# Five loads moved to the front of the load queue of an attention and MLP kernel

## The chip, the cores and the metric

The kernel runs on one core of a Trainium2 chip. The metric is device time in microseconds (us) of one execution: the median of three runs is 648.29 us (647.89 to 649.43). A further execution, the one that was profiled, took 646.66 us; durations in the text come from it.

## The reference

Attention with a soft cap over 4 batches, 12 heads, 448 positions and 64 numbers per head, then a two-layer MLP with a squared ReLU over the 1792 resulting rows (768 wide, 2048 in the middle):

```python
scores = scale * np.matmul(q, k.transpose(0, 1, 3, 2))
scores = cap * np.tanh(scores / cap)
scores = scores - np.max(scores, axis=-1, keepdims=True)
attn = np.exp(scores)
attn = attn / (np.sum(attn, axis=-1, keepdims=True) + 1e-09)
x = np.matmul(attn, v)              # then heads side by side: (1792, 768)
h = x @ w_in
r = np.maximum(h, 0.0)
out = (moe_s * (r * r) + moe_b) @ w_out
```

Everything is float32, `cap` is a scalar that comes from memory, and the result is (1792, 768) in float32.

## The kernel before

Two heads make a pair, and a batch has six pairs. For a pair the kernel loads k and q (128 x 448 float32, 224 KB each) and v (256 KB). TensorE computes scores in pieces of 128 keys for both heads (L514, four or eight matmuls into a `ps_s` buffer, of which there are two). ScalarE takes a piece through tanh (L518) and then exp (L522). The tanh needs the scale `tsc`, which VectorE computes from `cap` (L1163, L1164, the function `setup`). TensorE then multiplies the exponentials with v (L573) and with ones for the sums (L581), and ScalarE copies the result out of PSUM (L611).

The MLP weights are prepared in the same time. `w_in` is read in 24 chunks of 128 x 1024 32-bit words (512 KB, the halves of float64 numbers): the function `piece` joins the two words of each number into a float32. One of its steps goes either to ScalarE (one instruction at L687) or to VectorE (L681 and L682); the others, L675 and L678, are on VectorE. Sums of squares follow (L723 to L725) and, after all three chunks of a column group, small matmuls (L735), a VectorE step (L743 to L745) and a matmul that spreads its result over the lanes (L479). Later the weights are split into two float16 halves and multiplied with the attention output; that fills most of the run, but lies behind the part that this change touches.

The order of work is set by the class `Plan`. All operations are recorded with a duration and a rank; `emit` simulates the engines, picks at each step the operation that can start first, and writes the chosen indices to the list `out`. At the end it calls the operations in the order of `out`, so each engine's instructions stand in a fixed order and are run in it. All loads are issued by SyncE (SP) on one queue. Eight completion semaphores serve these transfers in turn, so that in the stretch treated here SP issues a load only after the eighth load before it has landed. The 16 DMA engines work through the queue in the order of issue, apart from small differences between them.

On TensorE six matmuls on a zeroed tile (L1191) come first, to give the engine work at the start; the scores of the first pair follow.

Of the kernel before, what the change touches and what calls it, by code (L numbers as in the profile page):

```python
# [23 lines left out]
class Plan:  # L24
# [55 lines left out]
    def emit(self):  # L80
# [40 lines left out]
        ran = [None] * n  # L121
# [45 lines left out]
        out = []  # L167
        todo = n
        while todo:
# [25 lines left out]
            t, i, e = best  # L195
# [41 lines left out]
                            free[q][x] = max(free[q][x], last[k] + 0.15)  # L237
            out.append(i)
            todo -= 1
        for i in out:  # L240
            self.ops[i][0][ran[i]][1]()


def arrange(units, at):

    key = {}
    for name, pre, _ in units:
# [4 lines left out]
CHOICE = {  # L252
    'bias': 3.969,
    'shy': {'DVE': 0.3, 'POOL': 0.5},
# [42 lines left out]
    'ahead': 0.3,  # L297
    'tail': 0.9,
    'expo': ('ACT', 'DVE'),
    'evac': ('ACT',),  # L300
    'sq': ('ACT', 'DVE', 'POOL'),
    'whi': ('ACT', 'DVE'),
# [990 lines left out]
```

## Time and profile before

| what | value |
|---|---|
| median of 3 runs | 648.29 us |
| the profiled execution | 646.66 us |
| its span, first to last instruction | 644.8 us |
| TensorE busy | 621.4 us, 96% |
| VectorE / ScalarE / GpSimd busy | 441.9 / 341.6 / 201.3 us |
| mean granted TensorE clock | 0.995 |

Some 1.9 us of the profiled execution lie outside its span. Times in the views count from the first instruction of the span. Busy shares are means over the whole run; this change concerns the first 30 us alone, where ScalarE and VectorE are nearly always busy and the DMA engines are too.

### The profile page before, as it was taken

Reading aid. Unit: us, or ns where it says so; the run is one execution under the profiler, and the core shown is the slowest. Engines: PE = TensorE matmul, PEld = TensorE weight load, DVE = VectorE, ACT = ScalarE, POOL = GpSimd, SP = SyncE. Lnnn points to the kernel's source line nnn. Section 1 sums busy time; section 2 is a strip of 40 time slices with the busy share of each in tenths; the row PEclk is TensorE's granted clock in tenths of the full one; section 3 lists DMA queues with packets and bytes.
Section 4 is the critical chain, followed back from the end, with each engine's and each line's share of the span. In section 5 each row is a group of like instructions: output and inputs, shape, how many; then the busy total and the mean of one; then the engine's idle time right before and its main releaser. Section 6 shows DMA issues by size and latency. Waiting matters only on the chain.

```text
span 644.8 us, 11247 instructions
## 1 busy us (share of the span) xinstructions
PE 621.4 (96%) x4308; PEld 327.6 (51%) x4308; DVE 441.9 (69%) x891; ACT 341.6 (53%) x459; POOL 201.3 (31%) x176
## 2 busy tenths in 40 slices
PE   4999999999999899989999999999999999999997
PEld 1333334344444333333444445555557996555997
DVE  4998888996887799798978691446667221666322
ACT  3999988966675478476668460314334001433100
POOL 2031434282571477566524320016014000010000
PEclk9999999999999999989999999999999999999999
DMA  8855644631614664764483424366012874100772
GB/s 294 314 145 190 232 121 152 215 124 60 214 28 134 218 202 137 243 190 139 146 307 132 160 103 156 127 228 222 3 32 76 263 257 146 49 1 1 225 239 80
DMA packets 54774, 101.67 MB, mean 158 GB/s; under 512 B 16192, under 2 KB 34752, under 8 KB 54720
## 3 DMA queue, kind: packets, MB, share of 16 engines
q1 hardware_dynamic: 54720, 100.95, 47.0%
q8 instruction: 34, 0.56, 0.3%
q14 instruction: 20, 0.16, 0.1%
HBM read 82.58 MB, written 18.17 MB: 156 GB/s over the span
## 4 chain that ended last, share of the span: by engine, by line
PE 76%; DMA 10%; DVE 7%; SPq 2%; POOL 2%; issue 2%; ACT 1%; POOLq 0%; ACTq 0%; DVEq 0%
PE ps_m L1031 9%; PE ps_v L573 7%; PE ps_s L514 7%; PE ps_s L1031 6%; PE ps_s L871 6%; PE ps_s L873 6%; PE ps_s L872 6%; PE ps_m L871 5%; PE ps_m L872 5%; PE ps_m L873 5%; PE ps_m L1122 4%; PE ps_m L1123 4%; PE ps_m L1124 4%; PE ps_v L581 3%; DMA w<-in_w_out 3%; DMA bed<-in_qT 2%
## 5 line engine op out<-in xcount | busy, mean ns | idle before, releaser
L1031 PEld LDWEIGHTS <-w 128*128 128x128 f16 x1008 | 96.6, 98 | 1.1
L518 ACT ACTIVATE bed<-ps_s,arena 128x896 f32<-128x896 f32 x84 | 81.2, 1004 | 21.7 <-PE ps_s L514 17.5
L514 PE MATMUL ps_s<-bed 64*128 64x448 f32 (+1 forms) x384 | 82.4, 592 | 9.8 <-DMA bed<-in_qT 6.8
L522 ACT ACTIVATE bed<-bed,par 128x896 f32<-128x896 f32 x84 | 85.6, 1042 | 0.4
L573 PE MATMUL ps_v<-bed 128*32 128x448 f32 x768 | 82.6, 552 | 0.8 <-ACT pw L611 0.7
L1123 PE MATMUL ps_m<-gt,w 128*128 128x448 f16 x192 | 67.7, 352 | 0.7 <-POOL gt L446 0.7
L871 PE MATMUL ps_m<-x,w 128*128 128x448 f16 x192 | 67.8, 353 | 0.2 <-DVE arena L640 0.2
L1122 PE MATMUL ps_m<-gt,w 128*128 128x448 f16 x192 | 67.8, 353 | 0.0
L871 PE MATMUL ps_s<-x,w 128*128 128x448 f16 x192 | 67.7, 352 | 0.0
L872 PE MATMUL ps_s<-x,w 128*128 128x448 f16 x192 | 67.7, 352 | 0.0
L1124 PE MATMUL ps_m<-gt,w 128*128 128x448 f16 x192 | 67.7, 352 | 0.0
L873 PE MATMUL ps_s<-x,w 128*128 128x448 f16 x192 | 67.7, 352 | 0.0
L872 PE MATMUL ps_m<-x,w 128*128 128x448 f16 x192 | 67.7, 352 | 0.0
L873 PE MATMUL ps_m<-x,w 128*128 128x448 f16 x192 | 67.7, 352 | 0.0
L966 ACT ACTIVATE pw<-ps_s,arena 128x448 f32<-128x448 f32 x32 | 20.2, 633 | 88.6 <-PE ps_s L873 88.3
L871 PEld LDWEIGHTS <-w 128*128 128x128 f16 x384 | 37.5, 98 | 40.4 <-issue 6.3
L514 PEld LDWEIGHTS ps_s<-bed 64*128 64x128 f32 (+1 forms) x384 | 27.9, 180 | 54.9 <-issue 25.9
L873 PEld LDWEIGHTS <-w 128*128 128x128 f16 x384 | 37.6, 98 | 35.1
L872 PEld LDWEIGHTS <-w 128*128 128x128 f16 x384 | 37.6, 98 | 33.5 <-issue 0.2
L446 POOL TENSOR_TENSOR bed<-bed 128x896 f32<-128x896 f32 (+2 forms) x25 | 45.5, 1821 | 6.2 <-PE ps_v L573 4.6
L573 PEld LDWEIGHTS ps_v<-bed 128*32 128x32 f32 x768 | 21.0, 110 | 49.7 <-issue 32.5
L445 DVE TENSOR_TENSOR pw<-pw 128x224 f32<-128x224 f32 x53 | 25.1, 494 | 27.5 <-ACT pw L970 24.9
(142 smaller groups left out, 1022.8 us busy)
## 6 DMA issues: line engine op xcount, KB each, us to landing
w<-w SPq DMA_DIRECT2D x48, 512.0 KB, 4.4
w<-in_w_out SPq DMA_DIRECT2D x24, 512.0 KB, 5.8
w<-ws SPq DMA_DIRECT2D x24, 512.0 KB, 4.7
w<-in_w_in SPq DMA_DIRECT2D x18, 512.0 KB, 5.6
bed<-in_v SPq DMA_DIRECT2D x24, 256.0 KB, 3.8
ws<-w SPq DMA_DIRECT2D x12, 512.0 KB, 3.3
bed<-in_kT SPq DMA_DIRECT2D x24, 224.0 KB, 3.7
bed<-in_qT SPq DMA_DIRECT2D x24, 224.0 KB, 3.9
```

The costliest lines, as they stand in the source:

```text
L446: "POOL": (0.1 + n * 0.00225, lambda: nc.gpsimd.tensor_tensor(dst(), a(), c(), op)),
L514: nc.tensor.matmul(P[kp][o, h, 0:S], keys, P[q][rows], start=True, stop=True)
L518: 1.01, rank, lambda: nc.scalar.activation(P[kh], P[kp][:, :, 0:S], AF.Tanh, scale=tsc[:, 0:1]),
L522: 1.04, rank, lambda: nc.scalar.activation(P[kh], P[kh], AF.Exp, scale=par[:, 0:1]), r=["par"], w=[kh],
L573: nc.tensor.matmul(P[kp][o, 0, 0:S], P[kv][:, c, o], prob(c, h), start=(c == 0), stop=(c == NC))
L871: nc.tensor.matmul(ps[:, 0:S], wh, x[:, 0], start=(c == 0), stop=False)
L872: nc.tensor.matmul(ps[:, 0:S], wh, x[:, 1], start=False, stop=False)
L873: nc.tensor.matmul(ps[:, 0:S], wl, x[:, 0], start=False, stop=(c == NP - 1))
L1031: nc.tensor.matmul(at(), w(g, zw), b(g, zb), start=g == 0 and x == 0, stop=g == n - 1 and x == 2,)
L1122: nc.tensor.matmul(ps[:, 0:S], wh, ghi[:, f], start=(f == 0), stop=False)
L1123: nc.tensor.matmul(ps[:, 0:S], wh, glo[:, f], start=False, stop=False)
L1124: nc.tensor.matmul(ps[:, 0:S], wl, ghi[:, f], start=False, stop=(f == NF - 1))
```

## The change

After the simulation, the loads of `cap` and of k and q of the first two pairs are called first, in that order, and then everything else in the order it had. The simulated schedule is not made again.

```diff
-        for i in out:
+        lead = [i for k in CHOICE["lead"] for i in out if k in self.ops[i][3] and ran[i] == "SP"]
+        for i in lead + [i for i in out if i not in lead]:
             self.ops[i][0][ran[i]][1]()
...
     'expo': ('ACT', 'DVE'),
+    'lead': (('par', 0), ('k', 0, 0), ('q', 0, 0), ('k', 0, 1), ('q', 0, 1)),
     'evac': ('ACT',),
```

The start of SP's queue before (`gt` holds the first chunks of w_in, `bed` k, q and v, `par` the three scalars):

```order
L667 DMA gt<-in_w_in 128x1024 x2
L496 DMA bed<-in_v 128x512 x2
L1168 DMA par<-in_cap 128x1
L490 DMA bed<-in_kT 128x448 x2
L492 DMA bed<-in_qT 128x448
L667 DMA gt<-in_w_in 128x1024
L492 DMA bed<-in_qT 128x448
L667 DMA gt<-in_w_in 128x1024
L1168 DMA par<-in_s 128x1
L1168 DMA par<-in_b 128x1
L667 DMA w<-in_w_in 128x1024 x3
```

And now (lines count two more here):

```order
L1170 DMA par<-in_cap 128x1
L492 DMA bed<-in_kT 128x448
L494 DMA bed<-in_qT 128x448
L492 DMA bed<-in_kT 128x448
L494 DMA bed<-in_qT 128x448
L669 DMA gt<-in_w_in 128x1024 x2
L498 DMA bed<-in_v 128x512 x2
L669 DMA gt<-in_w_in 128x1024 x2
L1170 DMA par<-in_s 128x1
L1170 DMA par<-in_b 128x1
L669 DMA w<-in_w_in 128x1024 x3
```

Five loads moved ahead of two w_in chunks and two v loads, and q of the second pair also ahead of the third w_in chunk. From the fourth w_in chunk on, the same loads stand in front of each load.

VectorE's queue before, at its start (`gt` w_in chunks, `arena` small values such as tsc):

```order
L681 TENSOR_SCALAR gt<-gt 128x512
L682 SCALAR_TENSOR_TENSOR gt<-gt 128x512
L675 TENSOR_SCALAR gt<-gt 128x512 x2
L678 SCALAR_TENSOR_TENSOR gt<-gt 128x512 x2
L1163 RECIPROCAL arena<-par 128x1
L1164 TENSOR_SCALAR arena<-arena 128x1
```

And now:

```order
L683 TENSOR_SCALAR gt<-gt 128x512
L684 SCALAR_TENSOR_TENSOR gt<-gt 128x512
L677 TENSOR_SCALAR gt<-gt 128x512 x2
L680 SCALAR_TENSOR_TENSOR gt<-gt 128x512 x2
L1165 RECIPROCAL arena<-par 128x1
L1166 TENSOR_SCALAR arena<-arena 128x1
```

Nothing moved: the two instructions that make tsc stand behind the work on the first two w_in chunks, as they did. The same holds for ScalarE, TensorE and GpSimd, whose queues are word for word those of before apart from line numbers; ScalarE's begins with this (`ps_s` scores):

```order
L689 ACTIVATE gt<-gt 128x512
L1183 ACTIVATE arena<-par 128x1
L520 ACTIVATE bed<-ps_s,arena 128x896
L689 ACTIVATE gt<-gt 128x512
L524 ACTIVATE bed<-bed,par 128x896
L520 ACTIVATE bed<-ps_s,arena 128x896 x2
```

The first tanh (L520 here, L518 before) has a step of the second w_in chunk ahead of it, and the first exp has a step of the fourth.

## Rows read from the trace of the kernel before

**Rows 1.** The chain that ended last, in time order, 0 to 100 us: start, us, what.

```profile
5.59 7.52 DMA bed<-in_qT
...
13.12 7.17 DMA gt<-in_w_in
...
27.94 0.16 PE ps_m L479
28.11 1.65 PE ps_v L573 x16
...
71.08 1.73 PE ps_s L514 x8
```

**Rows 2.** Timeline, cap's issue and ScalarE: start, us, engine, line, operation [idle before <-releaser].

```profile
2.59 0.43 SPq L1168 DMA_DIRECT2D par<-in_cap  x1
...
5.59 0.71 ACT L687 ACTIVATE gt<-gt 128x512 f32<-128x512 f32 x1 [3.58 <-DMA gt<-in_w_in]
...
9.46 0.20 ACT L1181 ACTIVATE arena<-par 128x1 f32<-128x1 f32 x1 [3.16 <-DMA par<-in_cap]
...
13.25 1.01 ACT L518 ACTIVATE bed<-ps_s,arena 128x896 f32<-128x896 f32 x1 [3.59 <-PE ps_s L514]
14.47 0.69 ACT L687 ACTIVATE gt<-gt 128x512 f32<-128x512 f32 x1 [0.21 <-DMA gt<-in_w_in]
15.06 1.02 ACT L522 ACTIVATE bed<-bed,par 128x896 f32<-128x896 f32 x1
16.00 1.87 ACT L518 ACTIVATE bed<-ps_s,arena 128x896 f32<-128x896 f32 x2
```

**Rows 3.** Timeline of VectorE, 0 to 21 us.

```profile
5.94 1.28 DVE L678 SCALAR_TENSOR_TENSOR gt<-gt 128x512 int32<-128x512 int32 x2
...
9.66 0.15 DVE L1164 TENSOR_SCALAR arena<-arena 128x1 f32<-128x1 f32 x1
...
12.53 0.43 DVE L681 TENSOR_SCALAR gt<-gt 128x512 f32<-128x512 f32 x1 [2.65 <-DMA gt<-in_w_in]
...
20.32 0.43 DVE L681 TENSOR_SCALAR gt<-gt 128x512 f32<-128x512 f32 x1 [0.37 <-DMA gt<-in_w_in]
```

**Rows 4.** Stretches of 1 us: window, PE, PEld, DVE, ACT, POOL busy, PEclk, DMA share, GB/s.

```profile
6.00:7.00 1.00, 0.00 (x0) 0.00 (x0) 1.00 (x3) 0.30 (x1) 0.30 (x1) 1.00 0.55 197
7.00:8.00 1.00, 0.00 (x0) 0.00 (x0) 0.23 (x1) 0.00 (x0) 1.00 (x1) 1.00 0.22 68
8.00:9.00 1.00, 0.00 (x0) 0.00 (x0) 0.00 (x0) 0.00 (x0) 0.12 (x1) 1.00 0.69 249
9.00:10.00 1.00, 0.00 (x0) 0.00 (x0) 0.38 (x3) 0.20 (x1) 0.00 (x0) 1.00 1.05 407
...
13.00:14.00 1.00, 1.00 (x6) 0.35 (x2) 1.00 (x2) 0.75 (x1) 0.00 (x0) 1.00 1.06 361
14.00:15.00 1.00, 1.00 (x4) 0.53 (x4) 0.97 (x3) 0.79 (x2) 0.17 (x1) 1.00 1.03 410
```

**Rows 5.** Timeline of TensorE, 0 to 28 us.

```profile
2.08 2.42 PE L1191 MATMUL ps_m<-w 128*128 128x448 f16 x6 [2.08 <-POOL w L1194]
11.35 4.85 PE L514 MATMUL ps_s<-bed 64*128 64x448 f32 x12 [6.85 <-DMA bed<-in_qT]
17.03 2.03 PE L514 MATMUL ps_s<-bed 64*64 64x448 f32 x12 [0.83 <-ACT bed L518]
...
27.94 0.16 PE L479 MATMUL ps_m<-brief,ones 128*128 128x1 bf16 x1 [0.30 <-DVE brief L745]
```

**Rows 6.** Timeline of TensorE, 217 to 230 us.

```profile
218.39 1.77 PE L514 MATMUL ps_s<-bed 64*128 64x448 f32 x8
...
225.03 3.36 PE L514 MATMUL ps_s<-bed 64*128 64x448 f32 x8
```

**Rows 7.** Stretches around the same place; columns as in rows 4.

```profile
222.00:225.00 3.00, 1.20 (x11) 0.47 (x11) 1.88 (x5) 0.83 (x2) 0.72 (x1) 0.99 0.65 114
225.00:228.30 3.30, 3.30 (x10) 1.20 (x9) 2.82 (x12) 3.30 (x6) 1.96 (x4) 0.50 0.31 106
```

## The prediction, made before the changed kernel ran

> **What bounds the kernel now.** I read the chain that ended last first, because it says which wait of the opening decides. Its opening is not ScalarE or the scores but the load queue: the load of the second pair's q lands at 13.11, this lets SP issue a w_in chunk at 13.12, which lands at 20.3 [rows 1], VectorE works on it and its followers without idle time to speak of, and then TensorE gets the small spreading matmul at 27.94 [rows 1]. From there to 72.8 the chain is TensorE alone, piece after piece without a wait. So the start of the kernel is worth exactly what it does to two things: when TensorE can run that matmul at 27.94, and how far TensorE has got with the work in front of it.
>
> The timelines of the three engines say how tight this is. TensorE ends six warm-up matmuls at 4.50, idles 6.85 us for the first pair's q, does twelve score matmuls from 11.35 to 16.20 and starts at 17.03 a stretch in which it has no idle time until 27.6; the wait for VectorE before the matmul at 27.94 is only 0.30 us [rows 5]. ScalarE starts the first tanh at 13.25, behind TensorE, but then runs a step of the fourth w_in chunk, for which it waits until 14.47, before the first exp at 15.06 and the second tanh at 16.00 [rows 2]. The second tanh frees the score buffer that TensorE waits for at 17.03. The reader should see here that the fourth w_in chunk, not the first q, sets ScalarE's pace from 14.47 on.
>
> Last, the stretches of 1 us show the DMA engines. From 9 us on they move 400 GB/s or more; from 6 to 9 us only 197, 68 and 249 [rows 4]. At 410 GB/s the missing 716 KB are 1.75 us. In the queue this hole lies between the v loads and the first k, at the place of the cap load, 128 pieces of 4 bytes. ScalarE got cap only at 9.46, although it was issued at 2.59 [rows 2].
>
> **The change, part by part.**
>
> 1. *What moves.* Cap (512 B) and four loads of 229,376 B go in front of 1.05 MB of w_in and 0.52 MB of v. Nothing is added, and no queue but SP's changes. At 400 GB/s the four loads are 2.3 us, the two w_in chunks 2.6 us.
>
> 2. *What cap costs in front.* The nearest rows bound it. Where it stands now the hole is 1.75 us. The two loads of the same shape for s and b, which pass between 13 and 14 us, cost 49 GB/s in one of these us, 0.12 us [rows 4]. I take the value of cap's own row: it is the same load, and it stays the first of the three scalars to be read. The hole then moves to the front and the queue as a whole is as late as before. [...]
>
> 3. *The first scores.* The first two w_in chunks, with nothing ahead of them, land by 5.59 [rows 2]. The first k and q are 0.46 MB in place of 1.05, so 1.5 us less, and have cap's 1.75 ahead: the first q lands near 5.59 - 1.5 + 1.75 = 5.8 instead of 11.35. Eight matmuls fill the two score buffers; at the pace of rows 5 (12 in 4.85) that is 3.2 us, to about 9.0. TensorE has its input almost 6 us earlier.
>
> 4. *Where this gain goes: the first tanh.* The tanh needs tsc, and tsc stands on VectorE behind the work on the first two w_in chunks. These now land behind cap and 0.92 MB: 5.59 + 1.75 + 2.3 = 9.6. VectorE needs from the second chunk's landing to the end of its work 5.59 to 7.22 = 1.63 us [rows 2, 3] and the two small instructions 0.35 us (from cap's landing at 9.46 to 9.81), so the tanh starts near 11.6. That is 1.7 us before 13.25, not almost 6.
>
> 5. *Where the rest goes: the fourth w_in chunk.* The same ten loads stand in front of it as before. With the hole kept it lands at 14.47 as before, ScalarE's step on it stays at 14.47, the exp at 15.06, the second tanh at 16.00, and TensorE's dense stretch at 17.03. The gain of point 4 turns into idle time on ScalarE: 0.0 us.
>
> 6. *VectorE.* The third w_in chunk now has the second q in front of it, 229 KB or 0.57 us, so VectorE starts on it at 13.1 instead of 12.53. It waits 0.37 us at 20.32 [rows 3], which takes up part; at most 0.2 us reach 27.9, and by point 7 TensorE is later than that: 0.0 us.
>
> 7. *TensorE's clock.* The twelve score matmuls before 17.03 are slow: 4.85 us, where the twelve after it take 2.03 [rows 5]. [...] After the change eight of them run from 5.8 to 9.0, then TensorE idles until the first tanh has freed a buffer at about 12.6, does four (1 to 2 us), and idles again to 17.03: in the eight us before the dense stretch it works about a fifth of the time. What such a stretch does is in the trace: from 222 to 225 us TensorE is busy 1.20 of 3.00 us, and the next 3.3 us are granted 0.50; eight score matmuls take 3.36 there against 1.77 a little earlier [rows 6, 7]. So I expect the dense stretch to begin at the lower level and to lose what that row lost, 3.36 - 1.77 = 1.6 us. Nothing hides it except the 0.30 us for which TensorE waits before 27.94. Cost 1.3 us, with bounds of 0.0 (the clock stays up) and 2.5 (all twelve matmuls from 17.03 at the slow pace, 4.85 - 2.03 = 2.8, less 0.3). [...]
>
> *Sum.* ScalarE 0.0, VectorE 0.0, TensorE +1.3: the profiled execution goes from 646.66 to 647.96. Its time lies 1.63 us under the median of the runs, so the median goes from 648.29 to 649.6. After 27.94 TensorE is the chain to 72.8 without a gap, so nothing gives the 1.3 us back there, and what follows waits for engines, not for a fixed time.
>
> **The rivals.**
>
> - *Cap is cheap in front.* If the hole came from cap's place behind four large loads, as s and b suggest, the queue is 1.75 us earlier from the start. The fourth w_in chunk lands at 12.7, the dense stretch starts at 15.3, still at the low clock: TensorE reaches the matmul at 27.6 - 1.75 + 1.6 = 27.5, VectorE is ready at 26. Against 27.94 that is -0.4 to -0.5: 647.8. For it: 0.12 us in rows 4 for two loads of this shape. Against it: these came after cap.
> - *The hole stays but the clock does not fall.* Eight early matmuls right after the warm-ups might lift it, and the four at 12 might hold it. Then all terms are zero: 648.3. Against it: after the sparse stretch from 222 to 225 it fell [rows 7].
> - *Both good*: the queue 1.75 us earlier and the clock up, also through VectorE's chain: 648.29 - 1.8 = 646.5; with a little of the slow v stretch gone too, 646.
> - *Worse: the dense stretch is slow for longer.* One mechanism: the slow pace lasts there as long as it did from 11.35 to 16.20, so that all twelve matmuls at 17.03 have it. Then the loss is 2.5: 650.8. It decides once the slow pace lasts beyond about 20.5 us. For it: those 4.85 us [rows 5]. Against it: the slow stretch at 225 was over after 3.3 us [rows 7].
> - *That the loads are not in front* can be left out: the queue in the section on the change shows them there.
>
> **How the numbers follow.** Chances: forecast (649.6) 0.45, cheap cap 0.25, clock up with the hole 0.14, both good 0.07, slow for longer 0.09. The bound for a difference is 0.3% or 1.94 us, about what a measurement of this kernel can tell from no change: below 646.35 faster, above 650.23 slower. Faster: about half of "both good", and a tenth of "cheap cap" and of the unknown behind it, where a shift also changes the two low-clock stretches later in the run (each worth some 1.6 us): 0.11. Slower: most of "slow for longer" and a sixth of the forecast: 0.16. The range reaches from "both good" to a little under "slow for longer": 646.5 to 650.7; the forecast's own is 648.6 to 650.2.
>
> **What would show it.** In the changed kernel's profile the first score matmuls start near 5.8 (near 4 if cap is cheap). The stretches of 1 us show a hole before 4 us in place of that from 6 to 9. The first tanh starts at 11.6 and is followed by 2 us of idle time until the fourth w_in chunk at 14.5; that wait is the core of the argument. The group of twelve score matmuls that begins near 17.0 takes 3 us or more in place of 2.03, and the spreading matmul stands near 29.2. I am wrong if that group takes 2.0 us, if ScalarE's step on the fourth chunk comes before 13, or if the time differs by more than the range for a reason that lies behind 30 us.

## The result, and the profile after

| kernel | median of its executions | lowest to highest | n |
|---|---|---|---|
| before | 648.58 us | 646.75 to 650.90 | 7 |
| changed | 653.56 us | 650.96 to 655.87 | 7 |

The ratio is 1.0068, 95% interval 1.0040 to 1.0097. The forecast was 649.6 with a range of 646.5 to 650.7: the sign was right, the size was not. Two later comparisons of the same two kernels gave smaller numbers, 1.0019 [0.9995, 1.0043] and 1.0030 [1.0006, 1.0055] (below). The differences of the medians are 4.98, 2.39 and 2.57 us, against +1.3 forecast, so two of the three are about twice the forecast and the first nearly four times. By the ratios they are smaller, +4.4, +1.2 and +1.9 us, and the interval of the second reaches below 1. So the first comparison misses the forecast clearly, while the changed kernel's medians in the two repeats (650.10 and 650.73) lie at the upper end of its range.

The profiled execution of the changed kernel took 650.96 us, span 649.2. First its chain that ended last, 0 to 100 us (start, us, what), which answers to [rows 1]:

```profile
5.78 8.52 DMA gt<-in_w_in
14.33 0.69 ACT gt L689
15.02 0.93 ACT bed L524
15.95 0.90 ACT bed L520
16.89 3.66 PE ps_s L516 x12
20.55 2.85 PE ps_v L575 x16
...
44.83 0.17 DVE arena L745
...
60.25 4.80 DMA w<-in_w_in
...
84.46 2.89 DMA bed<-zd
87.51 1.37 POOL num L448
88.91 0.63 DVE arena L462
89.56 0.18 DVE arena L631 x2
89.77 0.17 DVE brief L632
90.14 2.17 PE ps_s L516 x8
```

The chain no longer runs through VectorE's w_in chunk and the matmul at 27.94. It runs through the fourth w_in chunk, ScalarE, and then TensorE, whose twelve score matmuls take 3.66 us. At 44.83 it leaves TensorE for VectorE, goes on through a w_in chunk (60.25) and a row of transfers of row sums, of which `bed<-zd` is the last, and comes back to TensorE only at 90.14. The prediction had followed the chain to 72.8 and never looked at that place.

ScalarE of the changed kernel (timeline, idle time and its releaser in brackets), against [rows 2]:

```profile
12.50 1.01 ACT L520 ACTIVATE bed<-ps_s,arena 128x896 f32<-128x896 f32 x1 [1.30 <-DVE arena L1186]
14.33 0.69 ACT L689 ACTIVATE gt<-gt 128x512 f32<-128x512 f32 x1 [0.82 <-DMA gt<-in_w_in]
14.93 1.03 ACT L524 ACTIVATE bed<-bed,par 128x896 f32<-128x896 f32 x1
15.86 1.87 ACT L520 ACTIVATE bed<-ps_s,arena 128x896 f32<-128x896 f32 x2
```

The early scores are worth 0.75 us at the first tanh (13.25 before), which VectorE's tsc holds back, and 0.14 us at the fourth chunk (14.47 before), which the load queue holds back. That is the core of the argument, as forecast. In a second profile of the kernel before (b1_again, below) the two stand at 12.83 and 14.06, so the 0.14 us are less than what two executions of one kernel differ by. (The section on the time before has ScalarE and VectorE "nearly always busy" in the first 30 us; they are busy 18.73 and 19.95 us of them, and that idle time is where the early scores are lost.)

TensorE of the changed kernel, against [rows 5]:

```profile
5.17 3.36 PE L516 MATMUL ps_s<-bed 64*128 64x448 f32 x8 [0.66 <-DMA bed<-in_qT]
13.56 1.87 PE L516 MATMUL ps_s<-bed 64*128 64x448 f32 x4 [5.04 <-ACT bed L520]
16.89 3.66 PE L516 MATMUL ps_s<-bed 64*64 64x448 f32 x12 [1.47 <-ACT bed L520]
20.48 2.92 PE L575 MATMUL ps_v<-bed 128*32 128x448 f32 x16
...
24.09 1.77 PE L516 MATMUL ps_s<-bed 64*128 64x448 f32 x8
...
30.27 0.18 PE L481 MATMUL ps_m<-brief,ones 128*128 128x1 bf16 x1
```

The dense stretch (the matmuls that follow one another without idle time from 16.89 on) begins 0.14 us earlier than before (17.03), but its twelve score matmuls take 3.66 us in place of 2.03, and the sixteen v matmuls behind them 2.92 in place of 1.71. At 24.09 the pace is normal again. The spreading matmul is 2.33 us late (30.27 against 27.94).

VectorE, against [rows 3]:

```profile
12.25 0.15 DVE L1166 TENSOR_SCALAR arena<-arena 128x1 f32<-128x1 f32 x1
...
13.01 0.43 DVE L683 TENSOR_SCALAR gt<-gt 128x512 f32<-128x512 f32 x1 [0.55 <-DMA gt<-in_w_in]
...
20.98 0.43 DVE L683 TENSOR_SCALAR gt<-gt 128x512 f32<-128x512 f32 x1 [0.55 <-DMA gt<-in_w_in]
...
28.68 0.16 DVE L745 TENSOR_REDUCE arena<-ps_m 128x1 f32<-128x2 f32 x1 [0.53 <-PE ps_m L737]
```

VectorE gets the chunk at 20.98, 0.66 us later than at 20.32 before, and at 28.68 VectorE even waits for TensorE. So in this execution TensorE was the later of the two paths.

Stretches of 1 us (last columns: granted clock, DMA share, GB/s), against [rows 4]:

```profile
2.00:3.00 1.00, 0.92 (x3) 0.44 (x4) 0.00 (x0) 0.01 (x1) 0.02 (x1) 1.00 0.55 58
3.00:4.00 1.00, 1.00 (x5) 0.30 (x2) 0.00 (x0) 0.00 (x0) 0.00 (x0) 1.00 0.81 269
...
6.00:7.00 1.00, 1.00 (x6) 0.57 (x4) 0.00 (x0) 0.00 (x0) 0.00 (x0) 1.00 0.62 222
...
12.00:13.00 1.00, 0.00 (x0) 0.00 (x0) 0.43 (x4) 0.50 (x1) 1.00 (x1) 1.00 0.67 262
13.00:14.00 1.00, 0.44 (x2) 0.44 (x4) 0.95 (x2) 0.51 (x1) 0.04 (x1) 1.00 0.60 193
```

The hole at 6 to 9 us is gone from its place, and there are low rates at the front. But there is a second hole now, at 12 to 14 us, where s and b stand; before, they passed there with almost none. The forecast had only one. What the queue has moved from the start to 12 and to 14 us (last column: mean GB/s) puts a size on both. The kernel before, then the changed one:

```profile
0.00:12.00 12.00, 3.07 (x8) 1.27 (x10) 3.44 (x9) 2.19 (x3) 2.76 (x12) 1.00 0.72 258
0.00:14.00 14.00, 5.07 (x14) 2.01 (x14) 4.87 (x12) 2.94 (x4) 2.76 (x12) 1.00 0.77 277
```

```profile
0.00:12.00 12.00, 5.78 (x14) 2.01 (x14) 2.85 (x6) 2.05 (x3) 1.72 (x12) 1.00 0.80 271
0.00:14.00 14.00, 6.22 (x16) 2.45 (x18) 4.23 (x11) 3.06 (x4) 2.76 (x12) 1.00 0.78 265
```

By 12 us the changed kernel is 0.16 MB ahead of the kernel before, so cap costs less in front than where it stood; by 14 us it is 0.17 MB behind, so s and b have taken back 0.8 us.

### The profile page after: what moved, and what is told of

Same layout as the page of the kernel before. It is cut to its first block, busy times and chain, and to the rows that moved or that the text cites. A ratio compares the mean times of both kernels' runs of the same rounds, so it can differ in the third digit from the quotient of the medians.

```text
span 649.2 us, 11246 instructions
## 1 busy us (share of the span) xinstructions
PE 625.0 (96%) x4308; PEld 327.7 (50%) x4308; DVE 441.8 (68%) x891; ACT 341.6 (53%) x459; POOL 199.7 (31%) x176
## 4 chain that ended last, share of the span: by engine, by line
PE 73%; DMA 10%; DVE 8%; SPq 3%; POOL 2%; ACT 2%; issue 2%; POOLq 0%; DVEq 0%; ACTq 0%
PE ps_m L1033 9%; PE ps_s L1033 6%; PE ps_v L575 6%; PE ps_s L516 6%; PE ps_s L874 6%; PE ps_s L875 6%; PE ps_s L873 6%; PE ps_m L873 5%; PE ps_m L875 5%; PE ps_m L874 5%; PE ps_m L1124 4%; PE ps_m L1125 4%; PE ps_m L1126 4%; PE ps_v L583 2%; DMA zd<-cmp 2%; DVE w L457 2%
## 5 line engine op out<-in xcount | busy, mean ns | idle before, releaser
L520 ACT ACTIVATE bed<-ps_s,arena 128x896 f32<-128x896 f32 x84 | 81.3, 1003 | 20.9 <-PE ps_s L516 15.0
L516 PE MATMUL ps_s<-bed 64*128 64x448 f32 (+1 forms) x384 | 84.1, 605 | 7.9 <-ACT bed L520 7.2
L575 PE MATMUL ps_v<-bed 128*32 128x448 f32 x768 | 84.3, 561 | 2.3 <-ACT pw L613 2.2
```

What stands on the lines that cost most here:

```text
L516: nc.tensor.matmul(P[kp][o, h, 0:S], keys, P[q][rows], start=True, stop=True)
L520: 1.01, rank, lambda: nc.scalar.activation(P[kh], P[kp][:, :, 0:S], AF.Tanh, scale=tsc[:, 0:1]),
L575: nc.tensor.matmul(P[kp][o, 0, 0:S], P[kv][:, c, o], prob(c, h), start=(c == 0), stop=(c == NC))
```

## The experiments

In every table here, "spread" is the start of the spreading matmul of the opening (27.94 before), "batch end" that of the matmul of the same line at the end of the first batch (87.25 before) with TensorE's wait for it. A difference to 27.94 or 87.25 is one to the first profile of the kernel before.

**e1_fill: keep TensorE's clock up.** The changed kernel, with matmuls on a zeroed tile in two of TensorE's gaps:

```diff
+    'fill': {(0, 0, 1): 16, (0, 0, 2): 6},
...
+            for _ in range(CHOICE["fill"].get((bb, c2, c), 0)):
+                nc.tensor.matmul(P["warm"][:, 0:S], idle[:, 0:128], idle[:, 0:S], start=True, stop=True)
```

> The changed kernel, with 16 matmuls on the zeroed tile put on TensorE behind the second score piece and 6 behind the third, in the time in which it idles there (5.0 and 1.5 us). Clock theory (the loss at the start is TensorE's low clock in the stretch from 16.9): that stretch begins at the high level, its first 12 score matmuls take 2.0 us instead of 3.66, the spreading matmul stands at 28 instead of 30.34, and the median falls by at least 2.4 us, to 651 or below (against 653.6). Queue theory (the loss comes from the loads landing in another order): the stretch may be fast, but the spreading matmul stays near 30 and the median stays at 653.

Measured: 650.29 us, ratio 1.0031 [1.0005, 1.0056]. The dense stretch ran at the full pace from 16.85 (2.03 us for its twelve score matmuls), and yet the spreading matmul came at 28.98, 1.04 us late: it now waited 1.51 us for VectorE. The clock accounts for the last 1.3 us of the 2.33, not for the rest. The median is 3.3 us below the changed kernel's first one, as written down beforehand, but no lower than the medians of its repeats (650.10 and 650.73, below).

**e2_delay: the kernel before, with the dense stretch held back by 17 such matmuls.**

```diff
+    'fill': {(0, 0, 2): 17},
```

> The kernel before, its load order untouched, with 17 matmuls on the zeroed tile behind the third score piece, which hold up TensorE's dense stretch by some 2.5 us at the high clock. If a delay of TensorE at 17 us is all there is to the change and is handed on one to one: 651.1. If such a delay grows behind (the changed kernel is 2.6 late at 20 us and 4.4 to 5 late at the end): 653 to 654. If it is taken up by waits behind: below 650.

Measured: 652.13 us, ratio 1.0072 [1.0044, 1.0099]. The stretch began 2.47 us later and the spreading matmul 2.01 later, but the batch end was 4.87 us later (92.12, after a wait of 4.32). A delay in the opening does come out at the end; against the second profile of the kernel before (28.73 and 90.33, below) it is 1.22 us in the opening and 1.79 at the batch end.

**e3_cap: only cap in front.**

```diff
-    'lead': (('par', 0), ('k', 0, 0), ('q', 0, 0), ('k', 0, 1), ('q', 0, 1)),
+    'lead': (('par', 0),),
```

> Of the change only the load of cap in front; k and q stay where they were. My theory (the hole of 1.75 us belongs to the first cap load and moves with it; the clock is untouched because the first scores stay at about 11.3): 0 to +0.3 us against before, 648.3 to 649, dense stretch from 17.0 at the high clock. Rival (the load order as such costs): 650 or more. If cap in front is cheap: the first scores at 9.6, up to 1.75 us faster, 646.8.

Measured: 647.80 us, ratio 0.9998 [0.9976, 1.0020]. First scores at 9.99 (timeline of TensorE), spreading matmul at 27.35, which is 0.6 us earlier; a second hole (49 GB/s at 12 to 13 us).

```profile
9.99 4.85 PE L516 MATMUL ps_s<-bed 64*128 64x448 f32 x12 [5.49 <-DMA bed<-in_qT]
```

The time came out as my theory had it, the trace did not: I had the hole of 1.75 us move to the front with cap and the scores stay at 11.3. They came 1.36 us earlier, and the dense stretch 1.48 us earlier (15.55). Cap in front by itself costs little, as the rival "cap is cheap in front" has it; the second hole then takes part of the gain back.

**e4_nocap: only k and q in front.**

```diff
+    'lead': (('k', 0, 0), ('q', 0, 0), ('k', 0, 1), ('q', 0, 1)),
```

> Of the change only k and q of two pairs in front; cap stays behind the v loads. Clock theory: the first scores run at 4 to 7 us, TensorE idles to 13 or later, the dense stretch begins at the low clock, and the median is like the changed kernel's, 652 to 654. In addition cap lands 2.3 us later than in the kernel before, near 11.8, which by itself delays nothing since the first tanh waits for the second w_in chunk. Rival (cap in front is what costs): 649 or below.

Measured: 650.66 us, ratio 1.0040 [1.0009, 1.0070]. The dense stretch began at 17.50 at the low clock, the spreading matmul at 30.58. Here the granted clock shows it (the stretch in which the twelve score matmuls take 3.66 us, columns as in rows 4):

```profile
17.50:21.00 3.50, 3.50 (x12) 0.91 (x12) 3.43 (x8) 3.50 (x4) 0.00 (x0) 0.50 1.04 407
```

In the changed kernel the same twelve take the same 3.66 us. So the late opening comes with k and q, not with cap. The median, forecast at 652 to 654, was lower. Cap, the first scalar here, is issued only at 4.74 us, and yet the rate is down to 129 GB/s at 4 to 5: the scalars are not the only thing that lowers it.

**b1_again and a1_again: both kernels once more, unchanged.** No edit.

> The kernel before, unchanged, profiled once more. Its first profile was one of its faster executions (646.66; the median of 31 is 648.9). If the place at the end of the first batch, where TensorE waits for a chain of small loads (1.47 us there, at 87), varies by itself, this profile shows 2 to 4 us of wait there and perhaps a low-clock stretch behind it. If the longer waits of the changed kernels there (1.9 to 4.3 us) come from their shift, it shows 1.5 again.

> The changed kernel once more, timed beside the next two. Clock theory: dense stretch from 16.9 slow up to 20 or later, spreading matmul at 29 to 31, ratio near 1.006. If its first result was chance: ratio below 1.003.

Measured: the kernel before in one execution 651.51 us, the changed one 650.10 us, ratio 1.0019 [0.9995, 1.0043]. The profile of the unchanged kernel before is the surprise. Its opening was 0.79 us later than in the first profile (28.73), and its batch end 3.08 us later. In the opening the reason is the same slow pace, without any change to the loads:

```profile
16.62 3.60 PE L514 MATMUL ps_s<-bed 64*64 64x448 f32 x12 [0.85 <-ACT bed L518]
```

The twelve score matmuls take 3.60 us, not 2.03; only the v matmuls behind them run at the full pace (1.71). So the 2.03 from which the prediction counted belongs to one execution of the kernel before, not to all. The batch end of the kernel before in this repeat, then that of the changed kernel (timeline of TensorE):

```profile
90.33 0.16 PE L479 MATMUL ps_m<-brief,ones 128*128 128x1 bf16 x1 [3.75 <-DVE brief L630]
```

```profile
89.97 0.16 PE L481 MATMUL ps_m<-brief,ones 128*128 128x1 bf16 x1 [2.65 <-DVE brief L632]
```

At the batch end the two kernels stand within 0.4 us of each other. The first profile of before, on which the whole forecast rests, was an early one at this place. Behind its longer wait the repeat also has a stretch at the low clock, which the first profile has not:

```profile
92.00:95.00 3.00, 3.00 (x18) 0.79 (x20) 3.00 (x5) 2.74 (x5) 1.41 (x1) 0.50 0.44 148
```

From the batch end to the next spreading matmul the first profile takes 10.66 us, the repeat 12.30, the three profiles of the changed kernel 12.1 to 12.3. From there to the end of the span all five take 546.5 to 547.1 us. So what sets the first profile (span 644.8) apart from the other four (648.7 to 649.9) lies before 104 us, and the unchanged kernel's repeat has it too. Written down for a1_again was: near 1.006 if the first result holds, below 1.003 if it was chance. It was 1.0019.

**e5_actq: the order of before, but cap, s and b issued from ScalarE's queue.**

```diff
-    'lead': (('par', 0), ('k', 0, 0), ('q', 0, 0), ('k', 0, 1), ('q', 0, 1)),
+    'lead': (('par', 0), ('par', 1), ('par', 2)),
...
-            512, -80 + i if i else -100, lambda i=i, a=a: nc.sync.dma_start(par[:, i:i + 1], a.to_broadcast([128, 1])),
+            512, -80 + i if i else -100, lambda i=i, a=a: nc.scalar.dma_start(par[:, i:i + 1], a.to_broadcast([128, 1])),
```

> The kernel before with the loads of cap, s and b issued from ScalarE's queue at its start; SyncE's queue keeps its order without them. My theory (the hole of 1.75 us is the 4-byte pieces holding up the queue in which they stand): no hole from 6 to 9 us, first q at 9.6, fourth w_in chunk at 12.8, dense stretch from 15.3, spreading matmul near 26.2, median 1.5 us lower than before, 647.3. Rival (the hole is the DMA engines' own business, whatever the queue): hole stays in some place, median as before.

Measured: 652.45 us, ratio 1.0049 [1.0019, 1.0080]. The rate stayed at 143 to 205 GB/s from 2 to 6 us, where the kernel before has 262 to 356, and the spreading matmul came at 30.93. Here the small loads beside the large ones were worse than in line with them: what I expected of this run failed. The rate fell again, to 262 to 321 GB/s, from 11 to 15 us, which I can't explain.

**e6_actq_fill: k and q first, scalars on ScalarE's queue, fillers 16 and 10.**

```diff
+    'lead': (('par', 0), ('par', 1), ('par', 2), ('k', 0, 0), ('q', 0, 0), ('k', 0, 1), ('q', 0, 1)),
+    'fill': {(0, 0, 1): 16, (0, 0, 2): 10},
```

> k and q of two pairs in front as in the changed kernel, the three scalars from ScalarE's queue, and 16 and 10 matmuls on the zeroed tile behind the second and third score piece, to hold the clock up. Clock and queue theory together: no holes, dense stretch from about 15 at the high clock, spreading matmul near 26.5, median 1.5 us below before, 647.3. If holding the clock up and removing the holes does not make up for the order: 649 or more.

Measured: 649.10 us, ratio 1.0011 [0.9986, 1.0037]. No low-clock stretch by the granted clock in the whole profile, but the holes were not gone (120 to 135 GB/s from 2 to 6 us) and the dense stretch began at 17.12, not 15. Spreading matmul at 27.88, batch end at 88.92 with a wait of 3.21.

**e7_scalars: the three scalars in front, k and q at their old places.**

```diff
+    'lead': (('par', 0), ('par', 1), ('par', 2)),
```

> The order of the kernel before, with cap and the two activation scalars (three loads of 4 bytes a partition) in front of everything; k and q of the first pairs keep their places. Theory (each of these loads stops the stream of big loads wherever it stands, and loads that follow one another share one stop): one hole at 1 to 4 us and none at 12 to 14, where the kernel with cap alone in front shows 49 GB/s at 12 to 13; the fourth chunk of w_in lands 0.5 to 1.0 us earlier than in the kernel before, the first matmul that spreads the maxima comes 0.5 to 1.2 us earlier, and the median stands 0.5 to 1.5 us below the kernel before. Rival (small loads cost their queue the same wherever they are, each by itself): three stops in a row, k and q land later, no gain or +1. If the scatter behind 85 us is what decides, the ratio is within 0.3% of 1 whatever stands in front.

Measured: 649.44 us, ratio 1.0006 [0.9981, 1.0031]. There was one hole, at 3 to 5 us (29 and 99 GB/s), and none at 12 to 14, as the theory has it; but the fourth chunk still came at 14.50, and nothing was gained. The twelve score matmuls took 3.67 us here too, with k and q at their old places, and the spreading matmul came at 29.24. The part of my theory by which the three share one stop fell.

**e8_scalars_fill: e7's front with k and q, and the fillers of e6.**

> Cap, both scalars, k and q of the first two pairs in front, and 16 and 10 matmuls of a zero tile (results unused) behind the second and the third score piece, as in the earlier kernel with fillers. Theory (the change loses by TensorE's clock and by the second stop of the load stream): with both taken away the dense stretch begins at 16.5 to 17.1 us at the high clock, the spreading matmul at 27.3 to 28.0, and the median lies 0.3% or so below the changed kernel run beside it, at the kernel before or up to 1 us under it. Rival (the loss stands behind 85 us, in the wait for the small loads of the batch's end and the low clock after it): the trace shows the gain at 28 us and the time does not follow it.

Measured: 648.86 us, ratio 1.0010 [0.9987, 1.0033]; dense stretch at 17.78, spreading matmul at 28.94, each 0.7 to 0.9 us later than I had expected.

**a2_again and e9_fill_again: the changed kernel, and e1's kernel, side by side on one chip.**

> The changed kernel once more, to settle the size. If the first comparison (ratio 1.0068) held an accident of its few executions, this one repeats the second (1.0019): +0.5 to +2.5 us of medians. If the second was the accident, +3.5 to +5. In the trace: first tanh 12.3 to 12.6, dense stretch at 16.9 at the low clock, full clock at 21 to 23 us, spreading matmul at 29.4 to 30.4 us.

> The changed kernel with 16 and 6 matmuls of a zero tile (results unused) behind the second and third score piece, beside the changed kernel itself on one chip. Theory (TensorE's low clock in the first dense stretch costs 1.3 to 2.4 us): this kernel's median lies 1 to 2.5 us below that of the changed kernel. Rival (the lost time is made up or given away again behind 85 us): the two medians differ by less than 0.7 us. In the trace: dense stretch from 16.9 us with 12 score matmuls in about 2.0 us.

Measured: 650.73 us (1.0030 [1.0006, 1.0055]) and 650.58 us (1.0037 [1.0015, 1.0059]). TensorE with the fillers (timeline of e9_fill_again):

```profile
16.96 2.03 PE L517 MATMUL ps_s<-bed 64*64 64x448 f32 x12 [0.99 <-ACT bed L523]
18.93 1.71 PE L578 MATMUL ps_v<-bed 128*32 128x448 f32 x16
...
29.13 0.16 PE L482 MATMUL ps_m<-brief,ones 128*128 128x1 bf16 x1 [1.54 <-DVE brief L750]
```

VectorE of the same execution:

```profile
21.52 0.44 DVE L686 TENSOR_SCALAR gt<-gt 128x512 f32<-128x512 f32 x1 [0.92 <-DMA gt<-in_w_in]
```

The slow stretch is gone: 2.03 and 1.71 us, spreading matmul 1.39 us earlier than in a2_again (30.52). But the median moved by 0.15 us. The rival written beside it (given away again later) has the number. What holds the matmul here is the w_in chunk, which VectorE gets at 21.52 instead of 20.32: all of the 1.19 us by which 29.13 is late.

**e10_one, e11_one_fill, e12_one_only: the scalars as three pieces of 4 bytes instead of 384.** Each scalar goes to one lane, in front of all other loads, and a small matmul spreads them:

```diff
-            512, -80 + i if i else -100, lambda i=i, a=a: nc.sync.dma_start(par[:, i:i + 1], a.to_broadcast([128, 1])),
+            512, -80 + i if i else -100, lambda i=i, a=a: nc.sync.dma_start(lone[:, 128 + i:129 + i], a),
...
+        nc.vector.memset(lone[:, 0:128], 1.0)
+        nc.tensor.matmul(ps[:, 0:3], lone[:, 0:128], lone[:, 128:131], start=True, stop=True)
+        nc.vector.tensor_copy(par, ps[:, 0:3])
```

e10 has k and q in front too, e11 also the fillers 16 and 10, e12 leaves k and q where they were before.

> The changed kernel with the three scalars read as one piece of 4 bytes each into one lane, in front, and spread over the lanes by one small matmul (128x3) behind the warm-ups and a copy on VectorE. Theory (the 128 pieces of 4 bytes stop the load stream): no hole in the first 16 us, that is 380 GB/s or more in every 1-us stretch from 4 to 16 us; the fourth chunk's step on ScalarE at 12.5 to 13.3 in place of 14.3; dense stretch at 15.3 to 16.0 with the low clock, spreading matmul at 28.0 to 29.0 in place of 29.5 to 30.5, median 1 to 2 us under the changed kernel, so within 1 us of the kernel before. Rival (any small load stops the stream, however few its pieces): holes as in the changed kernel, no gain.

> The same, and 16 and 10 matmuls of a zero tile (results unused) behind the second and third score piece. Theory (what the change loses is the clock and the stops of the stream): both gone, dense stretch at 15.3 to 16.0 at the high clock, spreading matmul at 26.5 to 27.3, median 1 to 2 us below the kernel before. Rival (what is gained before 30 us is given away at the batch's end near 88 us): the trace shows the gain at 27 and the time is that of the kernel before or more.

> The kernel before, with k and q at their places; only the scalars are read as three pieces of 4 bytes in front and spread by the small matmul. Theory (128 pieces stop the stream): no hole at 6 to 9 us, first scores at 9.6 in place of 11.35, fourth chunk at 12.7, spreading matmul at 26.2 to 27, median 1 to 2 us below the kernel before. Rival (any small load stops it): a hole of 1 us or more at the front, times as with cap alone in front (ratio 0.9998).

Measured: 650.51 us (1.0033 [1.0012, 1.0053]), 651.18 us (1.0054 [1.0027, 1.0081]) and 649.53 us (1.0011 [0.9989, 1.0032]). For e10 and e11 the openings I expected failed: the dense stretch began at 17.27 and 17.96, not at 15.3 to 16.0, and the spreading matmul came at 30.61 and 28.53. e10 has no hole at 12 to 14 us, but 233 and 258 GB/s at 4 to 6, with k and q in front as in e4, and its fourth chunk came at 14.72. So the pieces are not what makes the opening with k and q in front late. The loads of the first 16 us, all of SP's queue: the kernel before, the changed kernel, and e12, one fence each:

```profile
DMA packets 2181, 4.69 MB, mean 293 GB/s; under 512 B 620, under 2 KB 1132, under 8 KB 2181
```

```profile
DMA packets 2132, 4.53 MB, mean 283 GB/s; under 512 B 611, under 2 KB 1123, under 8 KB 2132
```

```profile
DMA packets 1834, 4.99 MB, mean 312 GB/s; under 512 B 199, under 2 KB 712, under 8 KB 1834
```

Without the 384 pieces the queue has moved 0.30 MB more by 16 us, 0.7 us at 410 GB/s; the changed kernel has moved 0.16 MB less, 0.4 us. So the pieces do hold up the stream; e7 against e12 says it too, both with the three scalars in front and k and q in place: 29 and 99 GB/s at 3 to 5 us with the pieces, 332 and 361 without. e12 is the cleanest opening of all: VectorE gets the chunk that it had at 20.32 before at 19.11, the spreading matmul stands at 26.74. And its time is not better. TensorE of e12, the opening and the batch end:

```profile
26.74 0.16 PE L483 MATMUL ps_m<-brief,ones 128*128 128x1 bf16 x1 [0.19 <-DVE brief L751]
```

```profile
89.39 0.16 PE L483 MATMUL ps_m<-brief,ones 128*128 128x1 bf16 x1 [4.57 <-DVE brief L636]
```

TensorE came to the batch end earlier and waited 4.57 us there. The chain of e12 says for what:

```profile
67.35 6.88 DMA zd<-cmp
...
75.42 2.30 DMA cmp<-pw
77.74 1.11 DVE cmp L549
...
79.11 4.46 DMA zd<-cmp
...
84.21 2.79 DMA bed<-zd
```

These are four transfers that carry row sums, one after another: 3.5 KB (`zd<-cmp`), 1.8 KB (`cmp<-pw`) and 112 KB (`bed<-zd`). `zd<-cmp` alone takes 6.88 and 4.46 us. The stretches behind it (e12; columns as in rows 4) show a lower clock, where the first profile of before had 1.00 throughout (its repeat, above, had 0.50):

```profile
90.00:92.00 2.00, 2.00 (x8) 0.68 (x4) 1.86 (x7) 0.94 (x2) 0.00 (x0) 0.50 0.51 128
92.00:95.00 3.00, 3.00 (x26) 0.74 (x24) 3.00 (x5) 2.30 (x5) 1.33 (x1) 0.79 0.43 145
```

After its wait TensorE ran at 0.50, and the eight score matmuls from 89.49 took 3.02 us, where a group of eight takes 1.77 at the full pace. So the gain of the opening went into the wait, and the low clock was added.

All kernels by their openings (one profiled execution each; the last column is the difference of medians to the kernel before on the same chip, in us):

| kernel | k, q in front | twelve score, sixteen v matmuls (us) | spread | batch end (wait) | difference |
| --- | --- | --- | --- | --- | --- |
| before | no | 2.03, 1.71 | 27.94 | 87.25 (1.47) | 0 |
| before, again | no | 3.60, 1.71 | 28.73 | 90.33 (3.75) |  |
| e12_one_only | no | 2.03, 1.71 | 26.74 | 89.39 (4.57) | +1.2 |
| e3_cap | no | 2.03, 1.71 | 27.35 | 89.08 (3.89) | -1.1 |
| e7_scalars | no | 3.67, 1.71 | 29.24 | 89.66 (2.58) | +1.3 |
| e6_actq_fill | yes | 1.94, 1.71 | 27.88 | 88.92 (3.21) | +1.4 |
| e11_one_fill | yes | 2.06, 1.71 | 28.53 | 89.68 (3.30) | +2.8 |
| e8_scalars_fill | yes | 2.03, 1.71 | 28.94 | 89.41 (2.64) | +0.7 |
| e1_fill | yes | 2.03, 1.71 | 28.98 | 90.00 (3.18) | +1.4 |
| e9_fill_again | yes | 2.03, 1.71 | 29.13 | 89.63 (2.66) | +2.4 |
| changed, a1_again | yes | 3.67, 2.07 | 29.47 | 89.97 (2.65) | +2.4 |
| e2_delay | no | 1.94, 1.71 | 29.95 | 92.12 (4.32) | +3.2 |
| changed, first | yes | 3.66, 2.92 | 30.27 | 89.98 (1.86) | +5.0 |
| changed, a2_again | yes | 3.66, 2.95 | 30.52 | 91.08 (2.71) | +2.6 |
| e4_nocap | yes | 3.66, 2.62 | 30.58 | 92.00 (3.22) | +1.8 |
| e10_one | yes | 3.66, 2.88 | 30.61 | 91.47 (3.00) | +2.2 |
| e5_actq | no | 3.05, 2.28 | 30.93 | 92.41 (3.64) | +4.7 |

The openings differ by 4.2 us, the batch ends (the first profile apart) by 3.5. The three early openings (before 28 us, the first profile apart) wait 3.2 to 4.6 us at the batch end; the later ones wait 1.9 to 4.3, so an early opening tends to buy a longer wait, with exceptions. No version beats the kernel before beyond its interval.

## Why the prediction was wrong

Three steps failed: the size of point 7's term, the zero of point 6 together with point 2 on which it rests, and the sentence that closes the sum. The first two show in the opening; the third is why the end can't be read off the opening.

Points 1 and 3 held in the changed kernel's trace, point 4 in its direction (0.75 us gained at the first tanh, 1.7 forecast), and so did the times of point 5. The first q was forecast at 5.8 and the scores began at 5.17; the first tanh was forecast at 11.6 and came at 12.50, because the second chunk landed at 10.44 (ScalarE's step on it) in place of 9.6, while VectorE's work behind it took 1.70 us, near the 1.63 assumed; the fourth chunk was forecast at 14.47 and came at 14.33, the dense stretch at 17.03 and 16.89. The gain of six microseconds at the first scores is gone by 16.89, for the two reasons given. That the fourth chunk came on time was luck in part: point 2 has cap's hole move to the front in its full size, which e3 and the 0.16 MB by 12 us refute, and the second hole made up for it. (The reading that the engines move 400 GB/s or more from 9 us on leaves out the 361 at 13 to 14 in rows 4; nothing in the sum hangs on it.)

**Point 7 failed in its size.** The direction was right: the stretch began at the slow pace, 3.66 us for its twelve score matmuls, which in e4 goes with a granted clock of 0.50. I priced it by the row at 225 us, where eight matmuls lost 1.6 us, and stopped there. It lost 3.66 - 2.03 + 2.92 - 1.71 = 2.84 us, since the slow pace reached into the v matmuls, to about 23 us: the twelve lost the 1.6 us that I had, the v matmuls 1.2 more. My upper bound of 2.5 counted the score matmuls alone. In a1_again the spreading matmul was 1.53 us late and in a2_again 2.58: the end of the slow pace is not the same in each execution, and a single row does not tell where it lies. The other side of the difference is no constant either. I took the 2.03 us of one profile for the kernel before; its repeat has 3.60, and from that the changed kernel loses 3.66 - 3.60 + 2.92 - 1.71 = 1.27 us, and its spreading matmul is 0.74 to 1.79 us late. That the forecast of +1.3 lies in there is no credit to it, since it was worked out from the other profile.

**Point 6 failed too, hidden behind point 7.** I had VectorE late by 0.5 us at 13.1 (measured 13.01) and let its later idle time take it up: 0.0. But the next chunk, at 20.32 before, landed at 20.98, 21.16 and 20.96 in the three profiles of the changed kernel, and at 21.38 and 21.52 with fillers. With fillers everything on VectorE between there and the spreading matmul is back to back, so each of these delays arrives nearly in full: with the clock kept up the matmul was still 1.04 and 1.19 us late, and waited for VectorE. The step that failed is the sentence of point 2 that "the queue as a whole is as late as before". Cap's hole shrank when it moved, and s and b, which had cost 0.12 us, took 0.8 us more. A short distance behind cap does not make them cheap: in e4 it is shorter than before (cap's low rate, 140 GB/s, at 10 to 11 us, not at 7 to 8), and the rate still falls to 234 at 13 to 14. Nor is the second hole all of it: in e10, which has none, VectorE begins on that chunk at 20.77 without a wait, because the chunk before it came at 13.45. Why s and b were cheap in one place (0.12 us before) and not in the other (262 and 193 GB/s at 12 to 14 us of the changed kernel) stays open; no run here shows by what mechanism.

The two are parallel paths to one matmul. Against the first profile of before VectorE's gives about +1.1, TensorE's up to +2.6, and the later one counts.

**The closing sentence of the sum failed:** that what follows waits for engines, so that the delay stays as it is. TensorE waits at about 90 us for VectorE, mostly at the end of a chain of transfers of row sums that are issued among loads of 224 to 512 KB (in a1_again the chain there runs through ScalarE), and this wait was between 1.5 and 4.6 us. A delay or a gain of the opening is changed there: e2's +2.01 became +4.87, e12's -1.20 became +2.14 (both against the first profile of before, which was early there by 3.08 against its own repeat). Behind the wait a stretch at the low clock can follow (granted 0.50 at 92 to 95 us of b1_again, 1.00 there in the first profile of before), worth some 1.6 us (12.30 against 10.66). The kernel before has its own `bed<-zd` in its chain at 81.77, behind the 72.8 at which my reading of it ended. That is also why the forecast had too narrow a range: executions of the unchanged kernel run from 644.2 to 652.6 us over all comparisons.

What is shown: work in TensorE's gaps removes the slow dense stretch (all five kernels with fillers in these gaps take 1.9 to 2.1 us for its twelve score matmuls), and with k and q in front and no fillers it is there in all five profiles, 3.66 or 3.67 us and on into the v matmuls. It is not the change's alone: with the scalars on SP's queue, k and q in place and no fillers, two of five profiles have it (b1_again 3.60, e7 3.67), if only in the score matmuls. Why some of these have it and others not stays open. What is not shown: that the time of the changed kernel follows from it. Taking the slow stretch away in e9 left the median where it was. In the nine comparisons with k and q in front, the first one apart, the medians are 0.7 to 2.8 us over the kernel before, and the intervals of three of them (a1_again, e6, e8) reach below 1; with k and q in place and the scalars on SP's queue (e3, e7, e12) they are -1.1 to +1.3. Which of the places before 104 us carries that difference stays open: by the profiles the unchanged kernel's repeat (span 649.7) is as long as the changed kernel's three (648.7 to 649.9). Why the first comparison gave twice the difference of the two repeats stays open as well; its profiled execution, 650.96 us, was the fastest of its seven.

## What to carry to other kernels

When an input is brought forward, follow the next two things that its consumer needs (here tsc and the fourth chunk) before counting a gain, and look at what the engine that now works earlier does in the gap that this opens: its clock may be down when the dense work comes (here twelve score matmuls took 3.66 us, and 2.03 with the gap filled). Price such a low-clock stretch by all instructions until the pace is normal again, with a bound that reaches past the first group. And before saying that a delay stays as it is, take a second profile of the unchanged kernel: the places where it differs from the first (here the pace at 17 us and the wait at 90) are where small changes are lost or doubled, and a term may not be counted from one of the two profiles alone.

## What the runs showed of the hardware

- Scalars spread to 128 lanes by their loads (128 pieces of 4 bytes each) can hold up a stream of large loads: 68 GB/s at 7 to 8 us in the kernel before (one scalar), 29 and 99 at 3 to 5 us in e7 (three), where e12 with three single pieces of 4 bytes has 332 and 361. What they cost differs by place: s and b together 0.12 us in the kernel before, 0.9 us in the changed one (262 and 193 GB/s at 12 to 14, where 410 is usual), 49 GB/s at 12 to 13 in e3. Issued on a second queue they went with 143 to 205 GB/s for four microseconds (e5).
- The granted clock in the rows reads 1.00 in 17 to 23 us of the changed kernel, where the matmuls go at about half their pace (3.66 us for twelve); with fillers, in e1, it reads 1.00 too, at 2.03 us; in e4, with the same 3.66 us, it reads 0.50. So in these openings a 1.00 in that column stands beside both paces, and only the durations tell them apart.
- Transfers of 1.8 and 3.5 KB of row sums took 2.3 to 6.9 us from issue to landing at 67 to 84 us of e12, issued among loads of 224 to 512 KB, and TensorE then waited 4.57 us at the end of the batch.
